# Diagonal 64x64 and 32x32 TensorE tiles in the attention stage of a fused linear-attention and mixture-of-experts kernel, blocks stored without their zeros, and 27 block sets instead of 20

## The chip, the cores and the metric

The kernel runs on one core of a Trainium2 chip. The metric is the device time of one execution in microseconds (us). TensorE (PE) multiplies matrices and writes only to PSUM; VectorE (DVE), ScalarE (ACT) and GpSimd (POOL) do the element-wise work; SyncE (SP) issues most of the DMAs. Each engine works through its own instructions in the order in which they stand; the engines wait for one another through semaphores.

## The reference

```python
def _attn_ref(r, k, v, w, a, b):            # B, H, S, D = 4, 8, 768, 40
    state = zeros((B, H, D, D))
    for t in range(S):
        y[:, :, t] = einsum('bhd,bhde->bhe', rt, state)
        Sa = einsum('bhde,bhe->bhd', state, at)
        state = state * wt[:, :, None, :] - einsum('bhd,bhe->bhde', Sa, bt)
        state = state + einsum('bhd,bhe->bhde', vt, kt)
    return y

def _moe_ref(x, w_gate, w1, w2):            # x: 3072 x 320, 8 experts, F = 1024
    P = exp(x @ w_gate - max)               # then 8 rounds of row and column normalisation
    for e in range(E):
        out += P[:, e:e+1] * (maximum(x @ w1[e], 0) @ w2[e])
```

The output of the attention, 3072 tokens of 8 x 40 values, is the input of the mixture of experts.

## The kernel before

**Two stages.** `attention` computes the recurrence, and `body` goes on with the eight experts. The experts start from `xd`, a DRAM copy of the attention's output, and use the SBUF that the attention's pools release, in the order of the pools: `stg` and `x0` lie where the attention's inputs, the inversion buffers and the first block sets were, `hp` (results of the first expert layer) over the last sets, `x1` over what comes behind.

**The recurrence in chunks.** The 768 steps are cut into 12 chunks of 64 (index `c`), for 4 batches (`b`) of 4 head pairs (`p`). The two heads of a pair lie side by side: on partitions 0 to 39 and 64 to 103 for the 40 dimensions, on 0 to 63 and 64 to 127 for the 64 steps of a chunk. Inside a chunk the recurrence is a triangular system. Three kinds of work result:

- `prep(c, b)` depends on inputs alone: two scans on DVE (`q`, `gf`), products on POOL or DVE (`kb`, `ab`), products and transposes on PE (`ll`, `kt`), and copies by ACT into a *block set* that `recur` reads later. A set has `sx` (832 columns), `bb` (the negated `b` vectors, 416 columns) and `cc`. There are `NSX` = 20 sets, used in turn. Eight of them serve at first as staging buffers for inputs (`IN_SETS`) and for `kb` and `lt` (`KB_SETS`) of the first eight preps. `first_use` (L100) clears `bb` on POOL and copies an identity into `sx` on ACT.
- The inversion: for two chunks at a time, 128 triangular 32x32 blocks are inverted on DVE (`inv_diag`, `inv_off`, L181 to L210), one block on each partition. `ld`, `ud` and `nd` are DRAM tiles that carry the blocks to that layout and back. `tload` (L212) fetches the inverted blocks, and `tmat` (L233) merges two 32x32 inverses into one 64x64 inverse with two products, `gp` and `op`, and ACT copies between and behind them. `tt` holds the result for each pair as a 128x128 matrix with one 64x64 inverse for each head on its diagonal and zeros elsewhere.
- `recur(c, b)` (L250) is the sequential part: `av`, the mask into `f` (DVE), `xc`, copies into `x1` and `c1` (ACT), `pu` = `tt` times `x1` (PE, L287), the mask into `pm` (DVE, L289), `c2` = `bb` times `pm` (PE, L294), the sum `ws` (DVE, L296), and from it the output `y` and the state `z` for the next chunk (POOL), transposed by PE (`zt`) into `vz`. One `recur` is called a step here: 48 steps.

**Products in float32.** Each product of two float32 operands stands in the trace as two LDWEIGHTS and two MATMUL records: 192 products `pu` give 384 records. A transpose gives one.

**What sets the order.** All pieces get a due time in the list `ev` and are written in that order; a scheduler that goes by its own timing of the program then sets the order on each engine, until block `N_MAN` = 8 of the experts, from where the written order holds. So a changed tile or count shifts the order of other pieces too.

**Experts.** `layer1` forms its products in seven pieces (L564), `layer2` adds into PSUM (L629). `prep_w` splits weights, `prep_x` splits inputs (`xs`, `xt`, `xch`, `xcl`) on DVE, ACT and POOL. The first `prep_x` run beside the last steps of the recurrence.

Of the kernel before, what the change touches and what calls it, by code (L numbers as in the profile page):

```python
# [29 lines left out]
def attention(ctx, tc, d, xd, ps, pq, pt, gs, lg):  # L30
    nc = tc.nc
# [17 lines left out]
    NTB = 2  # L49
    sx_b, bb_b, cc_b = ([None] * NSX for _ in range(3))  # L50
    raws = {}
    for n in range(NCH * NB - NSX, NCH * NB):
        i, pool = n % NSX, sets[n - NCH * NB + NSX]
        if i in IN_SETS or i in KB_SETS:
            raw = pool.tile([128, 1252], F32, name=f"st{i}")
            raws[i] = raw
            sx_b[i] = raw[:, 0:832].rearrange("r (p h x) -> r p h x", h=2, x=104)
            bb_b[i] = raw[:, 832:1248].rearrange("r (p x) -> r p x", x=104)
            cc_b[i] = raw[0:R2, 1248:1252]
            continue  # L60
        sx_b[i] = pool.tile([128, NP, 2, 104], F32, name=f"sx{i}")
        bb_b[i] = pool.tile([128, NP, 104], F32, name=f"bb{i}")
        cc_b[i] = pool.tile([R2, NP], F32, name=f"cc{i}")
    tt_b = [const.tile([128, 4 * NP, 128], F32, name=f"tt{i}") for i in range(NTB)]
    td_b = [const.tile([128, 4 * NP + 1, 32], F32, name="td")]
    lg_b = [const.tile([128, 4 * NP, 64], F32, name="lg")]
# [4 lines left out]
    x1_b = [const.tile([128, NP, 128], F32, name=f"x1{i}") for i in range(2)]  # L71
# [13 lines left out]
    def clear():  # L85
        nc.gpsimd.memset(unf, 0.0)
        nc.gpsimd.memset(unf[:, 0:1024:33], 1.0)
        for t in vz_b + c1_b + lg_b:
            nc.vector.memset(t, 0.0)
        for t in rb_b + f_b:  # L90
            nc.vector.memset(t[96:128], 0.0)
        nc.vector.memset(td_b[0][:, 4 * NP], 0.0)
        for t in x1_b:
            nc.vector.memset(t[:, :, 104:128], 0.0)
        nc.vector.memset(kb1[96:128], 0.0)
        for t in tt_b:
            nc.gpsimd.memset(t, 0.0)
    fresh = set(range(NSX))

    def first_use(i):  # L100
        if i in fresh:
            fresh.discard(i)
            nc.gpsimd.memset(bb_b[i], 0.0)
# [12 lines left out]
    def prep(c, b, ld):  # L116
# [16 lines left out]
        nc.vector.tensor_tensor_scan(  # L133
            out=gf.rearrange("r p t -> r (p t)")[:, 259::-1], data0=inp[:, 260:0:-1],
# [3 lines left out]
        g = gf[0:R2, :, 64:0:-1]  # L138
        if cb < NKB:
            raw = raws[KB_SETS[cb % len(KB_SETS)]]  # L140
            kb = raw[0:R2, 0:512].rearrange("r (p k t) -> r p k t", p=NP, k=2)
# [32 lines left out]
        nc.scalar.copy(out=sx[0:64, :, :, 64:104], in_=kt[0:64, :, :, 0:40])  # L174
        nc.scalar.activation(out=bb[0:64, :, 0:40], in_=kt[64:128, :, 0, 0:40], func=AF.Copy, scale=-1.0)
        nc.scalar.activation(out=bb[64:128, :, 64:104], in_=kt[64:128, :, 1, 0:40], func=AF.Copy, scale=-1.0)
# [35 lines left out]
    def tload(c):  # L212
        tt = rot("tt", tt_b)
        tts[c] = tt
        ld, ud, nd = invs[GRP[c][0]]
        t1, t2, lb = td_b[0][0:64, 0:4 * NP], td_b[0][64:128, 0:4 * NP], lg_b[0][0:64]
        cc = GRP[c][1]
        q = [slice(h * 32, h * 32 + 32) for h in range(2)]
        u = [[slice(cc * 64 + blk * 32 + h * 16, cc * 64 + blk * 32 + h * 16 + 16) for h in range(2)]
             for blk in range(2)]  # L220
        for h in range(2):
            nc.sync.dma_start(out=lb[q[h], :, q[h]],
                              in_=ld[cc, 0:32].rearrange("j b p h s -> j (b p) h s")[:, :, h, 32:64])
        for h in range(2):
            nc.sync.dma_start(out=t1[q[h]], in_=nd[u[0][h]].rearrange("g j s -> j g s"))
        for h in range(2):
            nc.sync.dma_start(out=t2[q[h]], in_=ud[u[1][h]].rearrange("g j s -> j g s"))
        for h in range(2):
            for blk in range(2):
                r = slice(h * 64 + blk * 32, h * 64 + blk * 32 + 32)  # L230
                nc.sync.dma_start(out=tt[r, :, r], in_=ud[u[blk][h]].rearrange("g j s -> j g s"))

    def tmat(c, half):  # L233
        gl = slice(half * 8, half * 8 + 8)
        tt = tts[c][:, gl]
        gw = slice(half * 8, half * 8 + 9)
        t1, t2 = td_b[0][0:64, gw], td_b[0][64:128, gw]
        lb, gs = lg_b[0][0:64, gl], lg_b[0][64:128, gl]
        gp = pt.tile([64, 2 * NP + 1, 32], F32, name="gp", tag="pt")
        for p in range(2 * NP):  # L240
            nc.tensor.matmul(gp[:, p:p + 2], lhsT=lb[:, p], rhs=t1[:, p:p + 2], start=True, stop=True)
        nc.scalar.copy(out=gs[0:32, :, 0:32], in_=gp[0:32, 0:2 * NP])
        nc.scalar.copy(out=gs[32:64, :, 32:64], in_=gp[32:64, 0:2 * NP])
        op = pt.tile([64, 2 * NP + 1, 32], F32, name="op", tag="pt")
        for p in range(2 * NP):
            nc.tensor.matmul(op[:, p:p + 2], lhsT=gs[:, p], rhs=t2[:, p:p + 2], start=True, stop=True)
        nc.scalar.copy(out=tt[0:32, :, 32:64], in_=op[0:32, 0:2 * NP])
        nc.scalar.copy(out=tt[64:96, :, 96:128], in_=op[32:64, 0:2 * NP])

    def recur(c, b):  # L250
# [16 lines left out]
        for p in range(NP):  # L267
            nc.tensor.matmul(av[:, p], lhsT=vz[:, p], rhs=rb[:, p], start=True, stop=True)
# [10 lines left out]
        x1 = rot("x1", x1_b)  # L279
        c1 = rot("c1", c1_b)  # L280
# [4 lines left out]
        pu = ps.tile([128, NP, 128], F32, name="pu", tag="ps")  # L285
        for p in range(NP):
            nc.tensor.matmul(pu[:, p], lhsT=tts[c][:, b * NP + p], rhs=x1[:, p], start=True, stop=True)  # L287
        pm = wk.tile([128, NP, 104], F32, name="pm")
        nc.vector.tensor_tensor(out=pm, in0=pu[:, :, 0:104], in1=mask_p.unsqueeze(1).broadcast_to([128, NP, 104]),  # L289
                                op=ALU.mult)  # L290
        yield
        c2 = ps.tile([R2, NP, 104], F32, name="c2", tag="ps")
        for p in range(NP):
            nc.tensor.matmul(c2[:, p], lhsT=pp["bb"][:, p], rhs=pm[:, p], start=True, stop=True)  # L294
        ws = wk.tile([R2, NP, 104], F32, name="ws")
        nc.vector.tensor_tensor(out=ws, in0=c2, in1=c1, op=ALU.add)  # L296
# [45 lines left out]
    preps, invs, tts, gd, ys = {}, {}, {}, {}, {}  # L342
# [477 lines left out]
```

## Time and profile before

| | |
|---|---|
| median of 3 runs | 1844.17 us (1842.89 to 1850.96) |
| the profiled execution | 1846.42 us, of which the span of the profile is 1844.6 us |
| granted TensorE clock, mean | 0.969 |
| busy share of the span | PE 93%, DVE 76%, POOL 48%, ACT 46% |
| first `pu` of the recurrence | 110.8 us |
| last `c2` of the recurrence | 519.2 us |

The recurrence runs from 111 to 520 us, prepared in the first 110 us; the rest belongs to the experts. In the profile, L with a number is a line of the kernel, PEld are the weight loads of TensorE, `out<-in` are the names of the written and read tiles, and a number behind "idle before" is how long the engine stood still ahead of the group, with what released it. A matmul's row shows a length that includes its way through the array; how close products follow each other is read from their starts.

### The profile page before, as it was taken

How to read it: one execution, taken by the hardware profiler on the slowest of the kernel's cores; microseconds unless marked ns; L12 is line 12 of the kernel's file. 1: busy time of each engine (PE TensorE's matmuls, PEld its weight loads, DVE VectorE, ACT ScalarE, POOL GpSimd, SP SyncE). 2: the span in 40 equal slices, each digit the busy share in tenths (PEclk: the TensorE clock that was granted, in tenths of full speed). 3: DMA queues.
4: the chain of work that ended last, by engine and by line, in shares of the span. 5: the costliest groups of instructions: out<-in, count | busy, mean ns of one | idle time of the engine just before them, and what ended most of it. 6: DMA issues, size and time to landing. Idle time of an engine off the chain costs nothing.

```text
span 1844.6 us, 31499 instructions
## 1 busy us (share of the span) xinstructions
PE 1717.9 (93%) x11843; PEld 1684.3 (91%) x11843; DVE 1395.4 (76%) x2315; ACT 855.9 (46%) x1848; POOL 882.4 (48%) x848
## 2 busy tenths in 40 slices
PE   4478898888989999999999999999999999999999
PEld 4368788888878999999999999999999999999999
DVE  7877979777598868677776868977686877767675
ACT  6357576675643534344343433445343443425342
POOL 6545655441573618355371826007191744628170
PEclk8579899999999999999999999999999999999999
DMA  8477787885730102011110202201020111102001
GB/s 211 117 169 160 175 201 178 178 179 129 188 95 31 56 2 74 21 55 38 38 56 19 75 20 68 66 12 57 20 75 20 56 38 38 57 19 75 5 34 43
DMA packets 194957, 145.10 MB, mean 79 GB/s; under 512 B 143861, under 2 KB 171637, under 8 KB 194805
## 3 DMA queue, kind: packets, MB, share of 16 engines
q1 hardware_dynamic: 191125, 137.35, 28.6%
q10 hardware_dynamic: 3680, 5.74, 1.1%
q8 instruction: 94, 1.54, 0.4%
q14 instruction: 58, 0.48, 0.1%
HBM read 117.00 MB, written 26.04 MB: 78 GB/s over the span
## 4 chain that ended last, share of the span: by engine, by line
PE 72%; DVE 13%; DMA 4%; issue 3%; POOL 3%; ACT 1%; SPq 1%; DVEq 0%; ACTq 0%; POOLq 0%
PE op L629 36%; PE p L564 33%; DVE pr L193 2%; DVE gt L196 2%; DMA inp<-in_inp_dram 1%; DVE un L196 1%; DVE q L123 1%; POOL kb L147 1%; DVE gf L133 1%; PE xc L276 1%; PE ll L159 1%; DMA ld<-lt 1%; DMA xs<-xd 1%; POOL ab L154 1%; DVE sm L582 1%
## 5 line engine op out<-in xcount | busy, mean ns | idle before, releaser
L564 PE MATMUL p<-xch,wh 128*128 128x384 f32 (+1 forms) x1792 | 604.8, 339 | 9.5 <-DVE sm L582 5.6
L585 ACT ACTIVATE hh<-sm 128x384 fp32r<-128x384 f32 x512 | 269.4, 527 | 723.2 <-DVE sm L582 723.2
L629 PE MATMUL op<-wh,hh 128*128 128x320 f32 x1536 | 476.4, 311 | 1.0 <-ACT hh L585 0.9
L629 PE MATMUL op<-wl,hh 128*128 128x320 f32 x1536 | 474.2, 309 | 0.0
L629 PE MATMUL op<-wh,hl 128*128 128x320 f32 x1536 | 466.7, 309 | 0.8 <-DVE hl L588 0.8
L510 POOL TENSOR_TENSOR wl<-ws,wh 128x640 fp32r<-128x640 f32 x60 | 103.1, 1718 | 605.6 <-ACT wh L508 605.4
L588 DVE SCALAR_TENSOR_TENSOR hl<-sm,hh 128x384 fp32r<-128x384 f32 x512 | 373.4, 763 | 2.4 <-ACT hh L585 2.0
L564 PEld LDWEIGHTS p<-xch,wh 128*128 128x128 f32 (+1 forms) x1792 | 336.8, 188 | 13.7 <-DVE sm L582 6.8
L564 PE MATMUL p<-xcl,wh 128*128 128x384 f32 x896 | 302.2, 337 | 0.0
L564 PE MATMUL p<-xch,wl 128*128 128x384 f32 x896 | 301.5, 337 | 0.0
L629 PEld LDWEIGHTS op<-wh,hh 128*128 128x128 f32 x1536 | 289.9, 189 | 1.6 <-ACT hh L585 1.5
L629 PEld LDWEIGHTS op<-wl,hh 128*128 128x128 f32 x1536 | 290.7, 189 | 0.0
L629 PEld LDWEIGHTS op<-wh,hl 128*128 128x128 f32 x1536 | 286.4, 188 | 1.2 <-DVE hl L588 1.0
L582 DVE TENSOR_TENSOR sm<-p,u 128x384 f32<-128x384 f32 x384 | 233.0, 617 | 8.8
L582 DVE TENSOR_TENSOR sm<-p,p 128x384 f32<-128x384 f32 x128 | 71.3, 557 | 129.0 <-PE p L564 74.4
L564 PEld LDWEIGHTS p<-xcl,wh 128*128 128x128 f32 x896 | 168.4, 188 | 0.0
L564 PEld LDWEIGHTS p<-xch,wl 128*128 128x128 f32 x896 | 168.4, 188 | 0.0
L582 DVE TENSOR_TENSOR p<-p,p 128x384 f32<-128x384 f32 x128 | 71.1, 556 | 101.6 <-PE p L564 101.2
L582 DVE TENSOR_TENSOR u<-p,p 128x384 f32<-128x384 f32 x128 | 70.8, 553 | 57.2 <-PE p L564 56.0
L159 PE MATMUL ll<-ab,kb 128*128 128x128 f32 x336 | 60.8, 335 | 48.3 <-POOL ab L154 23.2
L518 POOL TENSOR_TENSOR wl<-ss,wh 128x512 fp32r<-128x512 f32 x60 | 89.7, 1495 | 30.1 <-ACT wh L515 25.9
L159 PEld LDWEIGHTS ll<-ab,kb 128*128 128x128 f32 x336 | 52.3, 237 | 54.1 <-POOL kb L147 27.2
(161 smaller groups left out, 2747.3 us busy)
## 6 DMA issues: line engine op xcount, KB each, us to landing
ws<-in_wts_dram SPq DMA_DIRECT2D x60, 832.0 KB
inp<-in_inp_dram SPq DMA_DIRECT2D x42, 450.2 KB
rb<-in_r_dram SPq DMA_DIRECT2D x48, 224.0 KB
gd<-gf SPq DMA_DIRECT2D x48, 113.8 KB
gr<-gd SPq DMA_DIRECT2D x48, 113.8 KB
vz<-in_v_dram SPq DMA_DIRECT2D x48, 112.0 KB
ld<-lt ACTq DMA_DIRECT2D x40, 128.0 KB
f<-in_vt_dram SPq DMA_DIRECT2D x48, 80.0 KB
```

What stands on the lines that cost most here:

```text
L123: nc.vector.tensor_tensor_scan(out=qf.rearrange("r p t -> r (p t)"), data0=inp[:, 0:260], data1=one65, initial=0.0, op0=ALU.mult, op1=ALU.add)
L133: nc.vector.tensor_tensor_scan(out=gf.rearrange("r p t -> r (p t)")[:, 259::-1], data0=inp[:, 260:0:-1], data1=g1.rearrange("r p t -> r (p ...
L159: nc.tensor.matmul(ll[:, p], lhsT=kb[:, p], rhs=ab[0:kb.shape[0], p], start=True, stop=True)
L193: nc.vector.tensor_tensor(out=prv, in0=a.unsqueeze(3).broadcast_to([nu, n_c, n_k, n_r]), in1=m.unsqueeze(1).broadcast_to([nu, n_c, n_k, n_ ...
L196: nc.vector.tensor_reduce(out=dst, in_=prv.rearrange("u c k r -> u c r k"), op=ALU.add, axis=AX.X)
L510: g.tensor_tensor(out=wl[:, 0:640], in0=raw[:, 256:896], in1=wh[:, 0:640], op=ALU.subtract)
L518: g.tensor_tensor(out=lv[:, 3:7], in0=so[:, :, 0], in1=hv[:, 3:7, 0], op=ALU.subtract)
L564: nc.tensor.matmul(o, lhsT=w_, rhs=x_, start=(j == 0), stop=(j == 3))
L582: eng.tensor_tensor(out=out, in0=x, in1=y, op=ALU.add)
L585: nc.scalar.activation(out=hh[:, f, h], in_=sm[f][:, h], func=AF.Relu)
L588: v.scalar_tensor_tensor(out=hl[:, f, h], in0=sm[f][:, h], scalar=0.0, in1=hh[:, f, h], op0=ALU.max, op1=ALU.subtract)
L629: nc.tensor.matmul(ops[i], lhsT=a[:, h, cs], rhs=w_[:, cw], start=(f == 0 and h == 0 and j == 0), stop=(last and h == 1 and j == 2))
```

## The change

**Products.** `pu` and `c2` were four products each over the full array, with block-diagonal weights. Each is now eight products, one for each head of each pair, with both operands on partitions 0 to 63 or 64 to 127 and the result on the same ones: the two tiles on the diagonal of TensorE. `gp` and `op` were eight 64x64 products each per half chunk (with two neighbours of `td` as moving operand); each is now sixteen 32x32 products.

**Storage.** With no block-diagonal weights, `tt` shrinks from 128 to 64 columns for a pair, `lg` from 64 to 32, `x1` from 128 to 104, and `bb` from 416 to 184 (160 of data and 24 that are cleared since the last head reads 64 columns). `gp` goes back with one ACT copy instead of two.

**Clearing.** `lg`, the spare column of `td` and the tail of `x1` are no longer cleared by DVE; `first_use` clears 24 columns instead of 416.

**Sets.** `NSX` is 27. The staging sets are now 19 to 26, so the preps of the first 19 sets write to memory that was no staging buffer.

```diff
-            raw = pool.tile([128, 1252], F32, name=f"st{i}")
+            raw = pool.tile([128, 1032], F32, name=f"st{i}")
...
+        else:
+            raw = pool.tile([128, 1020], F32, name=f"st{i}")
+        sx_b[i] = raw[:, 0:832].rearrange("r (p h x) -> r p h x", h=2, x=104)
+        bb_b[i] = raw[:, 832:1016]
+        cc_b[i] = raw[0:R2, 1016:1020]
+    tt_b = [const.tile([128, 4 * NP, 64], F32, name=f"tt{i}") for i in range(NTB)]
+    td_b = [const.tile([128, 4 * NP, 32], F32, name="td")]
+    lg_b = [const.tile([128, 4 * NP, 32], F32, name="lg")]
...
-        for t in vz_b + c1_b + lg_b:
+        for t in vz_b + c1_b:
             nc.vector.memset(t, 0.0)
...
-        nc.vector.memset(td_b[0][:, 4 * NP], 0.0)
-        for t in x1_b:
-            nc.vector.memset(t[:, :, 104:128], 0.0)
...
-            nc.gpsimd.memset(bb_b[i], 0.0)
+            nc.gpsimd.memset(bb_b[i][:, 160:184], 0.0)
...
         for p in range(2 * NP):
-            nc.tensor.matmul(gp[:, p:p + 2], lhsT=lb[:, p], rhs=t1[:, p:p + 2], start=True, stop=True)
-        nc.scalar.copy(out=gs[0:32, :, 0:32], in_=gp[0:32, 0:2 * NP])
-        nc.scalar.copy(out=gs[32:64, :, 32:64], in_=gp[32:64, 0:2 * NP])
+            for r in (0, 32):
+                nc.tensor.matmul(gp[r:r + 32, p], lhsT=lg[r:r + 32, p], rhs=td[r:r + 32, p], start=True, stop=True)
+        nc.scalar.copy(out=lg[64:128], in_=gp)
...
+            for h in range(2):
+                r = slice(64 + h * 32, 96 + h * 32)
+                nc.tensor.matmul(op[h * 64:h * 64 + 32, p], lhsT=lg[r, p], rhs=td[r, p], start=True, stop=True)
...
-            nc.tensor.matmul(pu[:, p], lhsT=tts[c][:, b * NP + p], rhs=x1[:, p], start=True, stop=True)
+            for h in hs:
+                nc.tensor.matmul(pu[h, p], lhsT=tts[c][h, b * NP + p], rhs=x1[h, p], start=True, stop=True)
...
-            nc.tensor.matmul(c2[:, p], lhsT=pp["bb"][:, p], rhs=pm[:, p], start=True, stop=True)
+            for h in hs:
+                nc.tensor.matmul(c2[h, p], lhsT=pp["bb"][h, p * 40:p * 40 + 64], rhs=pm[h, p], start=True, stop=True)
...
-NSX = 20
+NSX = 27
...
-IN_SETS = (19, 18, 17, 16)
-KB_SETS = (15, 14, 13, 12)
-IN_SEQ = (19,18,17,16,0,0,19,18)
+IN_SETS = (26, 25, 24, 23)
+KB_SETS = (22, 21, 20, 19)
+IN_SEQ = (26, 25, 24, 23, 0, 0, 26, 25)
```

**The order, on PE.** Near the end of the recurrence, where `gp` and `op` of the last chunk stand among the steps, PE had before (x4 is a group of four products; `lp` is the gate's product, `kt` and `ll` belong to a prep and are past):

```order
L316 MATMUL zt<-cst,z 40x104 x4
L326 MATMUL lp<-gs,y 128x8 x3
L294 MATMUL c_5164<-pm,bb_187 104x104 x4
L241 MATMUL gp<-td,lg 64x64 x8
L287 MATMUL pu<-x_213,tt_202 128x128 x4
L276 MATMUL xc_5183<-f_208,sx_192 104x104 x4
L276 MATMUL xc_5184<-f_208,sx_192 104x104 x4
L246 MATMUL op<-td,lg 64x64 x4
L268 MATMUL av<-rb_211,vz_217 104x128 x4
L246 MATMUL op<-td,lg 64x64 x4
```

and now, in the same part of the last chunks:

```order
L315 MATMUL zt<-cst,z 40x104 x4
L293 MATMUL c_5975<-pm,st_201 64x104 x8
L285 MATMUL pu<-x_218,tt_206 64x104 x7
L242 MATMUL op<-td,lg 32x32 x16
L285 MATMUL pu<-x_218,tt_206 64x104
L272 MATMUL xc_5999<-f_213,st_203 104x104 x4
L272 MATMUL xc_6000<-f_213,st_203 104x104 x4
L264 MATMUL av<-rb_216,vz_222 104x128 x4
```

The small products alone left the full array before; now `c2` and `pu`, which mostly follow each other, do so too. Over the whole attention stage the form of the tile changes 148 times before (74 stretches of 64x64) and 247 times now.

**The order, on POOL.** Among the preps of the first chunks, POOL had before:

```order
L154 TENSOR_TENSOR ab_205<-st_176,gf 40x4x64
L103 MEMSET st_170 128x416
L152 COPY cc_200<-q 104x4
L103 MEMSET st_169 128x416
L153 TENSOR_TENSOR ab_206<-st_175,gf 40x4x64
L154 TENSOR_TENSOR ab_206<-st_175,gf 40x4x64
L103 MEMSET st_176 128x416
L103 MEMSET st_172 128x416
L103 MEMSET st_175 128x416
L147 TENSOR_TENSOR kb<-st_175,q 104x512
```

and now:

```order
L149 TENSOR_TENSOR ab_209<-st_183,gf 40x4x64
L147 COPY st_191<-q 104x4
L98 MEMSET st_203 128x24
L148 TENSOR_TENSOR ab_210<-st_182,gf 40x4x64
L149 TENSOR_TENSOR ab_210<-st_182,gf 40x4x64
L98 MEMSET st_183 128x24
L98 MEMSET st_182 128x24
L98 MEMSET st_179 128x24
L142 TENSOR_TENSOR kb<-st_182,q 104x512
```

The place is the same; five clears of 416 columns ahead of `kb` have become four of 24.

**The order, on DVE.** Where the recurrence ends and the experts' inputs are prepared (`xt`, `xcl`, `xch` belong to `prep_x`), DVE had before:

```order
L269 TENSOR_TENSOR f_210<-av,cst 104x8x64
L296 TENSOR_TENSOR ws<-c_5288,c_222 104x416
L550 TENSOR_TENSOR xcl_5426<-xt,xch_5425 128x4x128
L552 TENSOR_TENSOR xch_5425<-xt,xch_5425 32x4x128
L289 TENSOR_TENSOR pm<-pu,cst 128x416
L330 COPY lg<-lp 128x8
L296 TENSOR_TENSOR ws<-c_5325,c_221 104x416
L582 TENSOR_TENSOR sm_5526<-p_5546,p_5528 128x384
```

and now:

```order
L549 TENSOR_TENSOR xcl_6191<-xt,xch_6190 128x4x128
L551 TENSOR_TENSOR xch_6190<-xt,xch_6190 32x4x128
L265 TENSOR_TENSOR f_214<-av,cst 104x8x64
L295 TENSOR_TENSOR ws<-c_6026,c_226 104x416
L287 TENSOR_TENSOR pm<-pu,cst 128x416
L329 COPY lg<-lp 128x8
L295 TENSOR_TENSOR ws<-c_6071,c_225 104x416
L287 TENSOR_TENSOR pm<-pu,cst 128x416
```

The last two operations of the first `prep_x` stand two places earlier, ahead of the last `f`. Elsewhere on DVE the inversions of chunks 2 and 3 end behind the third `ws` instead of the fifth, those of chunks 4 to 7 and of 10 and 11 one `ws` earlier than before, those of chunks 8 and 9 at the same one.

More of the change, by code (lines that the diff above doesn't have):

```diff
@@ L54, in attention @@
         if i in IN_SETS or i in KB_SETS:
-            raw = pool.tile([128, 1252], F32, name=f"st{i}")
+            raw = pool.tile([128, 1032], F32, name=f"st{i}")
             raws[i] = raw
[L57 to L66, printed above, removed]
+        else:
[6 more added lines that the diff above has]
+    lg_b = [const.tile([128, 4 * NP, 32], F32, name="lg")]
     ab_b = [pin.tile([128, NP, 128], F32, name=f"ab{i}") for i in range(2)]
@@ L70, in attention @@
     rb_b = [io.tile([128, NP, 128], F32, name=f"rb{i}") for i in range(NRB)]
-    x1_b = [const.tile([128, NP, 128], F32, name=f"x1{i}") for i in range(2)]
+    x1_b = [const.tile([128, NP, 104], F32, name=f"x1{i}") for i in range(2)]
     g1_b = [pin.tile([RP, NP, 65], F32, name=f"g1{i}") for i in range(1)]
@@ L174, in prep @@
         nc.scalar.copy(out=sx[0:64, :, :, 64:104], in_=kt[0:64, :, :, 0:40])
-        nc.scalar.activation(out=bb[0:64, :, 0:40], in_=kt[64:128, :, 0, 0:40], func=AF.Copy, scale=-1.0)
-        nc.scalar.activation(out=bb[64:128, :, 64:104], in_=kt[64:128, :, 1, 0:40], func=AF.Copy, scale=-1.0)
+        for h in range(2):
+            nc.scalar.activation(out=bb[h * 64:h * 64 + 64, 0:160].rearrange("s (p x) -> s p x", x=40),
+                                 in_=kt[64:128, :, h, 0:40], func=AF.Copy, scale=-1.0)
         if cb >= NKB:
@@ L215, in tload @@
         ld, ud, nd = invs[GRP[c][0]]
-        t1, t2, lb = td_b[0][0:64, 0:4 * NP], td_b[0][64:128, 0:4 * NP], lg_b[0][0:64]
+        t1, t2, lb = td_b[0][0:64], td_b[0][64:128], lg_b[0][0:64]
         cc = GRP[c][1]
@@ L221, in tload @@
         for h in range(2):
-            nc.sync.dma_start(out=lb[q[h], :, q[h]],
+            nc.sync.dma_start(out=lb[q[h]],
                               in_=ld[cc, 0:32].rearrange("j b p h s -> j (b p) h s")[:, :, h, 32:64])
@@ L229, in tload @@
             for blk in range(2):
-                r = slice(h * 64 + blk * 32, h * 64 + blk * 32 + 32)
-                nc.sync.dma_start(out=tt[r, :, r], in_=ud[u[blk][h]].rearrange("g j s -> j g s"))
+                nc.sync.dma_start(out=tt[h * 64 + blk * 32:h * 64 + blk * 32 + 32, :, blk * 32:blk * 32 + 32],
+                                  in_=ud[u[blk][h]].rearrange("g j s -> j g s"))
     def tmat(c, half):
@@ L235, in tmat @@
         tt = tts[c][:, gl]
[L236 to L239, printed above, removed]
+        td, lg = td_b[0][:, gl], lg_b[0][:, gl]
+        gp = pt.tile([64, 2 * NP, 32], F32, name="gp", tag="pt")
         for p in range(2 * NP):
-            nc.tensor.matmul(gp[:, p:p + 2], lhsT=lb[:, p], rhs=t1[:, p:p + 2], start=True, stop=True)
-        nc.scalar.copy(out=gs[0:32, :, 0:32], in_=gp[0:32, 0:2 * NP])
-        nc.scalar.copy(out=gs[32:64, :, 32:64], in_=gp[32:64, 0:2 * NP])
-        op = pt.tile([64, 2 * NP + 1, 32], F32, name="op", tag="pt")
+            for r in (0, 32):
+                nc.tensor.matmul(gp[r:r + 32, p], lhsT=lg[r:r + 32, p], rhs=td[r:r + 32, p], start=True, stop=True)
+        nc.scalar.copy(out=lg[64:128], in_=gp)
+        op = pt.tile([96, 2 * NP, 32], F32, name="op", tag="pt")
         for p in range(2 * NP):
-            nc.tensor.matmul(op[:, p:p + 2], lhsT=gs[:, p], rhs=t2[:, p:p + 2], start=True, stop=True)
-        nc.scalar.copy(out=tt[0:32, :, 32:64], in_=op[0:32, 0:2 * NP])
-        nc.scalar.copy(out=tt[64:96, :, 96:128], in_=op[32:64, 0:2 * NP])
+            for h in range(2):
+                r = slice(64 + h * 32, 96 + h * 32)
+                nc.tensor.matmul(op[h * 64:h * 64 + 32, p], lhsT=lg[r, p], rhs=td[r, p], start=True, stop=True)
+        for h in range(2):
+            nc.scalar.copy(out=tt[h * 64:h * 64 + 32, :, 32:64], in_=op[h * 64:h * 64 + 32])
     def recur(c, b):
@@ L284, in recur @@
         yield
-        pu = ps.tile([128, NP, 128], F32, name="pu", tag="ps")
+        pu = ps.tile([128, NP, 104], F32, name="pu", tag="ps")
+        hs = [slice(h * 64, h * 64 + 64) for h in range(2)]
         for p in range(NP):
-            nc.tensor.matmul(pu[:, p], lhsT=tts[c][:, b * NP + p], rhs=x1[:, p], start=True, stop=True)
+            for h in hs:
+                nc.tensor.matmul(pu[h, p], lhsT=tts[c][h, b * NP + p], rhs=x1[h, p], start=True, stop=True)
         pm = wk.tile([128, NP, 104], F32, name="pm")
-        nc.vector.tensor_tensor(out=pm, in0=pu[:, :, 0:104], in1=mask_p.unsqueeze(1).broadcast_to([128, NP, 104]),
+        nc.vector.tensor_tensor(out=pm, in0=pu, in1=mask_p.unsqueeze(1).broadcast_to([128, NP, 104]),
                                 op=ALU.mult)
         yield
-        c2 = ps.tile([R2, NP, 104], F32, name="c2", tag="ps")
+        c2 = ps.tile([128, NP, 104], F32, name="c2", tag="ps")
         for p in range(NP):
-            nc.tensor.matmul(c2[:, p], lhsT=pp["bb"][:, p], rhs=pm[:, p], start=True, stop=True)
+            for h in hs:
+                nc.tensor.matmul(c2[h, p], lhsT=pp["bb"][h, p * 40:p * 40 + 64], rhs=pm[h, p], start=True, stop=True)
         ws = wk.tile([R2, NP, 104], F32, name="ws")
-        nc.vector.tensor_tensor(out=ws, in0=c2, in1=c1, op=ALU.add)
+        nc.vector.tensor_tensor(out=ws, in0=c2[0:R2], in1=c1, op=ALU.add)
         if b % 2 == 0:
```

## The prediction

> **What bounds the kernel now.** I read the table by stages first, since the average hides that the program has two.
>
> ```profile
> span 1844.6 us, 31499 instructions
> ...
> core 0: us, PE busy (x) PEld busy (x) DVE busy (x) ACT busy (x) POOL busy (x), PEclk, DMA share, GB/s
> 184.00:230.00 46.00, 38.40 (x341) 35.76 (x340) 42.28 (x61) 26.84 (x67) 27.76 (x28) 0.89 0.77 176
> 322.00:368.00 46.00, 40.47 (x392) 38.17 (x390) 35.67 (x58) 30.31 (x77) 19.95 (x25) 0.93 0.85 180
> 368.00:415.00 47.00, 41.45 (x413) 38.53 (x412) 33.25 (x57) 33.22 (x84) 23.66 (x27) 1.00 0.81 175
> 600.00:1844.00 1244.00, 1238.63 (x7778) 1236.36 (x7776) 919.36 (x1577) 502.57 (x990) 571.42 (x491) 1.00 0.13 42
> ```
>
> From 600 us on PE is busy 1238.6 of 1244 us, at the full granted clock (1.00). The change touches nothing there, so whatever it does happens in the first 520 us. In the recurrence two engines take turns. From 184 to 230 us, where an inversion runs, DVE is busy 42 of 46 us (92%); from 322 to 415 us DVE falls to 71 to 78% and PE stands at 88%. The chain of waits, second, agrees:
>
> ```profile
> by line: issue 10.2%; DVE pr L193 7.3%; DVE gt L196 6.8%; DMA inp<-in_inp_dram 6.3%; DVE un L196 5.7%; POOL kb L147 3.9%; DVE q L123 3.9%; PE xc L276 3.4%; DVE gf L133 3.1%; PE ll L159 2.5%; DVE pm L289 2.4%; DVE ws L296 2.2%; PE av L268 2.
> ```
>
> Between 110 and 521 us its largest engine entries are the inversion (L193 and the two of L196, 19.8% together); of PE's products `xc`, `ll` and `av` appear, each under 4%, and `pu`, `c2`, `gp`, `op` not at all. So I let half of a PE saving or loss in the recurrence reach the end.
>
> **Products: the pace.** Third comes one stretch in order of time in which PE never pauses, with ACT's copy of `gp` ahead and one `gp` group from elsewhere behind:
>
> ```profile
> L243 ACT COPY lg<-gp 32x256 f32<-32x256 f32 x24 | 8.7, 362 | 0.3
> ...
> 388.15 1.04 PE L268 MATMUL av<-rb,vz 128*104 128x128 f32 x8
> 389.03 0.52 PE L316 MATMUL zt<-cst,z 104*40 104x104 f32 x4
> 389.39 0.90 PE L294 MATMUL c<-pm,bb 128*104 128x104 f32 x8
> 390.12 1.08 PE L159 MATMUL ll<-ab,kb 128*128 128x128 f32 x8
> 391.03 0.52 PE L167 MATMUL kt<-cst,kb 104*128 104x104 f32 x4
> 391.39 1.08 PE L287 MATMUL pu<-x,tt 128*128 128x128 f32 x8
> 392.31 1.63 PE L276 MATMUL xc<-f,sx 128*104 128x104 f32 x16
> 393.77 1.04 PE L268 MATMUL av<-rb,vz 128*104 128x128 f32 x8
> 394.74 0.68 PE L241 MATMUL gp<-td,lg 64*64 64x64 f32 x8
> 395.34 1.16 PE L159 MATMUL ll<-ab,kb 128*128 128x128 f32 x8
> 396.34 0.52 PE L167 MATMUL kt<-cst,kb 104*128 104x104 f32 x4
> ...
> 174.85 1.11 PE L241 MATMUL gp<-td,lg 64*64 64x64 f32 x16
> 175.89 0.98 PE L276 MATMUL xc<-f,sx 128*104 128x104 f32 x8
> ```
>
> From start to start, 8 records of `pu` (128 columns) take 392.31 - 391.39 = 0.92 us, 0.115 each; 8 of `c2` (104 columns) 390.12 - 389.39 = 0.73, 0.091 each. For `gp` (64 columns) 8 take 0.60 and 16 take 1.04 us, so 8 more cost 0.44, 0.055 each. The pace follows the columns.
>
> **Do two tiles run at once?** The change doubles the records: 16 for each `pu` and each `c2`, 32 for each `gp` and `op` of a half chunk. One place bears on it: at 109 us `op` (partitions 64 to 127) and `gp` (0 to 63) met.
>
> ```profile
> 108.38 0.97 PE L246 MATMUL op<-td,lg 64*64 64x64 f32 x13
> 109.13 0.27 PE L241 MATMUL gp<-td,lg 64*64 64x64 f32 x1
> 109.18 0.22 PE L246 MATMUL op<-td,lg 64*64 64x64 f32 x1
> 109.24 0.22 PE L241 MATMUL gp<-td,lg 64*64 64x64 f32 x1
> 109.24 0.22 PE L246 MATMUL op<-td,lg 64*64 64x64 f32 x1
> 109.30 0.22 PE L241 MATMUL gp<-td,lg 64*64 64x64 f32 x1
> 109.30 0.22 PE L246 MATMUL op<-td,lg 64*64 64x64 f32 x1
> 109.35 0.92 PE L241 MATMUL gp<-td,lg 64*64 64x64 f32 x13
> ```
>
> Two records start at 109.24 and two at 109.30: each tile keeps its pace of 0.055 to 0.06 us while the other runs. So I take two diagonal tiles as two streams.
>
> - `pu`: 8 records a stream at the pace of 104 columns, 8 x 0.091 = 0.73 instead of 0.92 us; 48 times -0.19 is **-9 us of PE**.
> - `c2`: 0.73 as before, **0**.
> - `gp`, `op`: 16 records a stream. If the pace goes on falling with the columns, 32 columns take 0.0275 us, 0.44 for a group instead of 0.88; if the pair at 109.24 is already the fastest issue (two in 0.058), 32 records take 0.93. I take the middle, 0.69, since the column law has three rows and the issue limit one; 48 groups times -0.19 is **-9**, between -21 and +2.
>
> The Trainium skill (TensorEngine Tiling (Array Packing), Gotcha 1: PSUM Pressure) says that different row tiles cannot write the same PSUM bank at a time. The two that met above wrote two banks; the diagonal pairs write one, on different partitions, which no row here shows. It is the rival "single file" below.
>
> **What the change of form costs.** The same stretch gives it. `av` ahead of `gp` lasts 394.74 - 393.77 = 0.97 instead of 389.03 - 388.15 = 0.88 us; the `gp` group 0.60 instead of 0.44; `ll` behind it 396.34 - 395.34 = 1.00 instead of 391.03 - 390.12 = 0.91. One stay in the 64x64 form costs 0.09 + 0.16 + 0.09 = 0.34 us, 0.17 a change. The form changes 148 times before and 247 times now: 99 x 0.17 = **+17 us of PE**. A direct step from 32 to 64 (47 of them) may cost less; with those at nothing it is (247 - 47 - 148) x 0.17 = +9.
>
> The Trainium skill (TensorEngine Tiling (Array Packing), Key Properties) says that changing the tiling mode drains TensorE. The rows agree and give the price, 0.17 us.
>
> PE together: -9 + 0 - 9 + 17 = -1 us, between -9 - 21 + 9 = -21 and -9 + 2 + 17 = +10. Half of it reaches the end: **-0.5**, between -10.5 and +5.
>
> **The start.** Until the first `q` everything waits for DVE's clears, then POOL stands ahead of a prep.
>
> ```profile
> 5.46 0.91 DVE L89 MEMSET lg<- 128x1024 f32 x1 [0.16 <-issue]
> 6.52 1.02 DVE L91 MEMSET rb<- 32x512 f32 x2
> 10.24 0.09 DVE L92 MEMSET td<- 128x32 f32 x1
> 10.68 0.48 DVE L95 MEMSET kb<- 32x512 f32 x1
> 11.20 0.70 DVE L123 TENSOR_TENSOR_SCAN q<-st,cst 112x260 f32<-112x260 f32 x1
> L123 DVEq EVENT_SEMAPHORE  x1: 21/21/21, 6.5 to 6.5; - x1
> 13.74 0.42 ACT L174 COPY sx<-kt 64x320 f32<-64x320 f32 x1 [5.05 <-PE kt L167]
> ...
> 9.73 0.21 POOL L466 MEMSET ones<- 128x128 f32 x1
> 40.10 0.45 POOL L103 MEMSET st<- 128x416 f32 x1
> 41.00 0.83 POOL L103 MEMSET st<- 128x416 f32 x2 [0.46 <-DMA ld<-st]
> 41.91 1.18 POOL L147 TENSOR_TENSOR kb<-st,q 104x512 f32<-104x512 f32 x1
> ```
>
> Without `lg`, `td` and `x1`, DVE saves (6.52 - 5.46) + (10.68 - 10.24) = 1.5 us ahead of `q`, whose semaphore event is over at 6.5 us, so nothing else holds it. On POOL a clear of 416 columns takes 0.45 us; one of 24 lies below the 0.21 of 128 columns, so the three ahead of `kb` at 41.9 us save about 0.9, less what the wait for `ld` (0.46) keeps: between 0 and 1.3, I take **1**. In sum **-2.5**, between -1 and -2.8. Seven more identity copies on ACT cost nothing while ACT waits for the first transposes, 5 us long.
>
> **ACT and the hand-over.** `gp`'s copy is one instead of two: 24 x 0.36 = 8.7 us of ACT. With 33 of 47 us busy at most, ACT hides most of that, between 0 and -2: **-1**. Two operations of `prep_x` stand ahead of the last `f` now instead of behind two later pieces; the same work in another order, 0, between -2 and +2 (its two operations take under 2 us). The 27 sets: no wait of a prep for a released set is among the listed waits of the recurrence, so **0** from the memory itself. The span that the order shifts is at most a step, 409 us / 48 = 8.5 us.
>
> **Sum.** 1844.6 - 0.5 - 2.5 - 1 = 1840.6 us of span. The profiled execution is 1846.4 by the metric, 2.2 above the median of the runs; -4 from the median 1844.2 gives **1840 us**. A change under 0.5%, 9.2 us, cannot be told from none here.
>
> **The rivals.**
>
> - *Cheap small tiles.* `gp` and `op` go on at the column pace and direct steps between 32 and 64 cost nothing: PE -21, and the stretches of 322 to 415 us pass half on: 1844 - 10.5 - 3.5 = **1830**. For it: the pace falls evenly over three widths. Against it: the chain names none of these products.
> - *A step gained by the order.* Four of five inversions end one or two `ws` earlier in DVE's order. If the recurrence waits for them at one place, a step goes: 1840 - 8.5 = **1832**. For it: 20% of the chain are inversions. Against it: DVE has the same work, and what is put behind comes later.
> - *Single file.* The pairs share a PSUM bank and run one after the other. `pu` takes 16 x 0.091 = 1.46 (+0.54), `c2` +0.73, 48 times 1.27 = +61; with +17 of changes and nothing gained at `gp` PE has +78 us more; half is +39: 1844 + 39 - 3.5 = **1880**, slower. It decides as soon as a second tile's record starts 0.09 instead of under 0.01 us behind the first. For it: no row shows one bank. Against it: the streams at 109 us.
> - *The changes on the path.* Each step now holds a change into and out of the 64x64 form between `x1` and `ws`, which the step's own chain waits for: all +17 reaches the end, the shorter `pu` and `gp` stay hidden: 1844 + 17 - 3.5 = **1857**. For it: PE at 88% and its long gaps rather than its pace would have to hide them. Against it: half of the recurrence hangs on DVE.
>
> **How the numbers follow.** Forecast 46%, its own range 1832 to 1850; cheap small tiles 19%; order 10%; single file 11%; changes on the path 14%. Faster than 1835: most of the second and third and a tenth of the first, 0.31. Slower than 1853.4: the single file, two thirds of the last case, a little of the first, 0.21. Within: 0.48. The range takes in everything but the single file and the ends of the others: **1826 to 1857**.
>
> **What would show it.** Right: `pu` and `c2` of 16 records in about 0.75 us each from start to start, with two records starting together; a stay costing about 0.3 us; the first `q` near 9.7 us; a first expert product as late as before within 5 us. Wrong: 1.4 us for a group (single file); groups of `gp` of 0.45 us (cheap tiles); inversions that start several us earlier while PE's groups are as forecast (order); PE's pauses of the recurrence unchanged but its busy time up by 15 us (changes on the path). After 600 us the profile should be the same as before; if it is not, the forecast has missed a whole part.

## The result: 0.7% slower, and the profile after

The changed kernel takes 1861.46 us (median of 6 runs, 1857.49 to 1865.25) against 1848.70 us of the kernel before in the same comparison (6 runs, 1842.89 to 1850.96): ratio 1.0074, interval 1.0053 to 1.0095, so 12.8 us slower. The forecast was 1840 us, range 1826 to 1857; it started from the median of three runs of the kernel before, 1844.17 us, which lies 4.5 us below that of the six.

The table by stages of the changed kernel, same columns as the one of before:

```profile
span 1858.7 us, 34584 instructions
...
core 0: us, PE busy (x) PEld busy (x) DVE busy (x) ACT busy (x) POOL busy (x), PEclk, DMA share, GB/s
184.00:230.00 46.00, 39.06 (x557) 34.97 (x556) 43.12 (x67) 30.50 (x77) 26.68 (x32) 0.93 0.80 182
322.00:368.00 46.00, 36.44 (x496) 33.35 (x495) 31.47 (x57) 30.34 (x77) 23.04 (x29) 0.93 0.86 187
368.00:415.00 47.00, 39.53 (x537) 36.06 (x537) 33.73 (x45) 29.41 (x75) 21.53 (x24) 0.86 0.70 162
600.00:1844.00 1244.00, 1241.01 (x7790) 1238.95 (x7790) 923.77 (x1588) 504.28 (x994) 572.09 (x492) 1.00 0.13 42
```

From 600 us on nothing has changed: PE is as full as before (1241.0 of 1244 us), at full clock. The span has grown by 14.1 us, and the sum `ws` that ends each step says where; the view of one tile gives count, shortest/median/longest ns, and first and last start, first of before, then of after:

```profile
L296 DVE TENSOR_TENSOR ws<-c,c x48: 549/582/620, 120.0 to 519.5; 104x416 f32<-104x416 f32 x48
```

```profile
L295 DVE TENSOR_TENSOR ws<-c,c x48: 555/584/601, 130.9 to 532.8; 104x416 f32<-104x416 f32 x48
```

The recurrence begins 10.9 us late and ends 13.3 us late. The products are not the reason. Here is PE in the changed kernel without a pause, with most of a `gp` group near the top:

```profile
388.56 1.12 PE L264 MATMUL av<-rb,vz 128*104 128x128 f32 x8
389.61 0.43 PE L236 MATMUL gp<-td,lg 32*32 32x32 f32 x14
389.97 0.54 PE L315 MATMUL zt<-cst,z 104*40 104x104 f32 x4
390.44 0.93 PE L293 MATMUL c<-pm,st 64*64 64x104 f32 x16
391.20 0.88 PE L285 MATMUL pu<-x,tt 64*64 64x104 f32 x16
392.01 0.69 PE L242 MATMUL op<-td,lg 32*32 32x32 f32 x32
```

From start to start 16 records of `c2` take 0.76 us (8 took 0.73 before), 16 of `pu` 0.81 (8 took 0.92), and 32 of `op` are over within 0.69 us, where 16 took 1.04 and more. So two tiles run at once, and a record of 32 columns costs about 0.02 us. The medians over all groups that run on without a pause at full clock, worked out from the starts and with the changes of form in them, went from 0.73 to 0.76 us for `c2`, 0.97 to 0.81 for `pu`, 1.07 to 0.62 for `op`: 48 times (+0.03 - 0.16 - 0.45) is **28 us less work for PE** in these groups (`gp` and `op` are 48 together, and `gp` is put down like `op`). Of the groups beside them `zt` alone grew clearly, from 0.36 to 0.45 us, which takes some 4 us back over its 44 groups.

What grew is DVE's idle time. The windows of the recurrence for DVE alone, before (110 to 520 us) and after (110 to 533 us); behind the length stand its busy time and its instructions:

```profile
110.00:520.00 410.00, 323.37 (x479) 0.95 0.74 172
```

```profile
110.00:533.00 423.00, 320.26 (x473) 0.89 0.72 167
```

The work is the same, 323 and 320 us; the idle time went from 86.6 to 102.7 us. The waits of DVE in the same stretches, before and then after (us in total, times, longest):

```profile
DVE f L269 <- PE av L268: 26.3, 11, 5.6
DVE pr L184 <- DMA lu<-ld: 13.2, 4, 5.2
DVE ws L296 <- PE c L294: 11.8, 13, 1.7
DVE q L123 <- DMA inp<-in_inp_dram: 9.4, 5, 3.9
```

```profile
DVE f L265 <- PE av L264: 31.2, 16, 6.4
DVE ws L295 <- PE c L293: 18.5, 16, 2.4
DVE q L118 <- DMA inp<-in_inp_dram: 14.9, 5, 5.6
DVE lg L329 <- PE lp L325: 11.1, 10, 4.2
DVE st L164 <- PE ll L154: 8.7, 7, 1.8
```

The inversions no longer wait for their DMA (13.2 us gone), and most of the others wait more. Shorter products that are waited for longer point to where the instructions stand. At the start this can be seen on DVE, before and after:

```profile
113.80 1.54 DVE L133 TENSOR_TENSOR_SCAN gf<-inp,g 112x260 f32<-112x260 f32 x1
115.26 0.56 DVE L289 TENSOR_TENSOR pm<-pu,cst 128x416 f32<-128x416 f32 x1
```

```profile
113.45 1.53 DVE L128 TENSOR_TENSOR_SCAN gf<-inp,g 112x260 f32<-112x260 f32 x1
...
120.00 1.08 DVE L192 TENSOR_REDUCE gt<-pr 128x64 f32<-128x512 f32 x1
120.99 0.59 DVE L287 TENSOR_TENSOR pm<-pu,cst 128x416 f32<-128x416 f32 x1
```

The first `pm` stood right behind `gf`; now eight pieces of the second inversion and the `q`, `g` and `gf` of a prep stand between them. A second difference is the granted clock. The windows of 110 to 535 us, before and after:

```profile
110.00:535.00 425.00, 367.68 (x3430) 343.72 (x3428) 337.26 (x497) 277.30 (x680) 219.37 (x242) 0.96 0.73 170
```

```profile
110.00:535.00 425.00, 360.28 (x4847) 325.80 (x4847) 321.83 (x476) 258.89 (x638) 200.97 (x234) 0.89 0.72 166
```

In these traces the granted clock is 1.00 or 0.50 and nothing between, so a mean of 0.96 is 2 x 0.04 x 425 = 34 us at half clock, 0.89 is 94 us (a mean of two digits leaves 4 us open either way). Two theories: **order** (the scheduler laid the pieces out anew, and the new order is the slower one) and **clock** (lighter products let TensorE fall to half clock more often, which gives the saving back).

### The profile page after: what moved, and what is told of

It reads as the page before. It is cut to its first block, busy times and chain, and to the rows that moved or that the text cites. A ratio compares the mean times of both kernels' runs of the same rounds, so it can differ in the third digit from the quotient of the medians.

```text
span 1858.7 us, 34584 instructions
## 1 busy us (share of the span) xinstructions
PE 1721.5 (93%) x13379; PEld 1675.7 (90%) x13379; DVE 1395.5 (75%) x2311; ACT 849.3 (46%) x1831; POOL 865.4 (47%) x855
## 4 chain that ended last, share of the span: by engine, by line
PE 73%; DVE 10%; DMA 6%; issue 4%; POOL 3%; SPq 2%; ACT 2%; POOLq 0%; DVEq 0%; ACTq 0%
PE op L628 35%; PE p L563 33%; DVE pr L189 1%; DVE gt L192 1%; DMA xs<-xd 1%; DVE un L192 1%; DVE gf L128 1%; DMA ld<-lt 1%; PE xc L272 1%; POOL ab L148 1%; DMA inp<-in_inp_dram 1%; PE ll L154 1%; DVE q L118 1%; PE c L293 1%; PE pu L285 1%
```

## The experiments

All ratios are to the kernel before, with the 95% interval. To set an order, a table of instruction numbers was added behind the program, with a dependency without a semaphore from each instruction to the next on its engine; the instructions themselves stay those of the changed kernel:

```diff
         body(tc, d, out)
+        _set_order(tc, nc)    # all five engines, one list each
```

### The change in the order of the kernel before

> The changed kernel's instructions, put on every engine into the order that the kernel before had. Theory 'order' (the 13 us were lost because the scheduler laid the pieces out anew, the first step's mask pm behind pieces of the second inversion above all): last ws back at 519 us or earlier, first ws near 120 us, time 1838 to 1849 us (ratio 0.994 to 1.000). Theory 'clock' (the lighter products leave TensorE idle in more of the clock's windows, and the half clock gives the saving back, whatever the order): half-clock time within the recurrence stays near 90 us (before 41), time 1855 to 1866 us.

Measured: 1850.58 us, ratio 1.0009 (0.9995 to 1.0022). So the order makes 10.9 us of the loss: that much lies between the same instructions in the two orders. Its steps run as those of before, on a lighter PE and a slower clock; first the view of `ws`, then the windows of all engines:

```profile
L295 DVE TENSOR_TENSOR ws<-c,c x48: 552/582/593, 120.7 to 522.2; 104x416 f32<-104x416 f32 x48
```

```profile
110.00:535.00 425.00, 369.83 (x4913) 334.10 (x4911) 334.66 (x495) 267.59 (x654) 216.93 (x240) 0.90 0.72 170
```

The first `ws` comes at 120.7 us (before 120.0), and the 41st at 469.2 (before 470.3): 28 us less of PE's work and 85 instead of 34 us at half clock leave the steps where they were. The last comes 2.7 us later. PE's busy time did not fall here, 369.8 after 367.7 us: the slower clock took up what the lighter products saved. So this run alone does not show that time on PE is worth nothing. The time is 1.6 us above what 'order' expected and 4.4 below 'clock'; the half-clock time is what 'clock' said. So the order has most of it, and whether the clock has the rest is the next question.

### Filling TensorE's waits, in both orders

In 38 and 35 places where TensorE had stood still for 0.8 us or more, products of the identity were put ahead, written into the tile that the next real product overwrites:

```diff
+    def warm(name, tile, m, n, sub=""):
+        ...
+        for _ in range(WARM.get(f"{name}{seen[name]}{sub}", 0)):
+            nc.tensor.matmul(tile, lhsT=ident[:, 0:m], rhs=ident[:, 0:n], start=True, stop=True)
...
+        warm("av", av[:, 0], 104, 128)
         for p in range(NP):
             nc.tensor.matmul(av[:, p], lhsT=vz[:, p], rhs=rb[:, p], start=True, stop=True)
```

> The changed kernel in its own order, with 226 products that nobody reads (about 51 us at full clock) in 38 places where TensorE stood still for 0.8 us or more between 112 and 535 us. Theory 'clock': half-clock time in the recurrence falls from 92 us to 60 or less, last ws at 518 to 526 us, time 1846 to 1855 us. Theory 'order': the waits have other causes than the clock, so the recurrence ends at 532 us or later, time 1858 to 1868 us.

> The change in the order of the kernel before (1850.6 us), with 160 products that nobody reads (some 36 us at full clock) in 35 places where TensorE stood still for 0.8 us or more between 112 and 525 us. If the half clock costs time there: half-clock time between 110 and 535 us falls from 89 to 50 us or less, and time to 1842 to 1847 us. If it is only a sign of waiting: 1849 to 1854 us.

Measured: 1866.45 us (1.0104, 1.0089 to 1.0120) in the change's order, and 1850.66 us (1.0014, 1.0001 to 1.0027) in the old one. The windows of 110 to 535 us of the first, then of the second:

```profile
110.00:535.00 425.00, 390.14 (x5296) 356.92 (x5296) 319.34 (x477) 259.02 (x638) 198.06 (x234) 0.95 0.72 166
```

```profile
110.00:535.00 425.00, 382.49 (x5224) 347.35 (x5224) 339.23 (x496) 268.34 (x655) 224.32 (x244) 0.96 0.72 170
```

The clock came back to that of before (0.95 and 0.96; 43 and 34 us at half clock). The time did not: 5 us more in the new order, nothing in the old one (1850.66 against 1850.58). The half clock was a sign of waiting, not what cost the time. In the second run PE is busy for 382.5 us, of which some 36 are fillers: about 21 us less of the kernel's own work than before, at the same clock, and by the medians the end did not come earlier. One limit: the fillers are not pure, since some wait themselves for the PSUM tile that they write (those ahead of `av` 9.0 us in the first run). The second run's profiled execution has a span of 1842.0 us, 6.7 less than that without fillers, but the medians of 12 and 11 runs agree: a single profiled execution lies some us off the median either way.

### Where in the order the loss is made

Two kernels change the order at the end of the second inversion: old order first, then the change's, and the reverse.

```diff
 # the second kernel is the reverse, with 156 us
-the change's order on every engine
+what the kernel before had begun by 166 us, in its order; then the rest in the change's order
```

> The changed kernel with the order of the kernel before up to the end of the second inversion (166 us), and its own order from there on. If the loss is made at the start (first ws at 130.9 instead of 120.0 us) and carried to the end: first ws near 120 us, time 1846 to 1853 us. If it is made by the later order or by the clock: 1857 to 1865 us.

> The reverse: the changed kernel's own order up to the end of the second inversion (156 us), then the order of the kernel before. If the loss is made at the start: first ws near 131 us, time 1857 to 1864 us. If by the later order: 1845 to 1852 us. Theory 'clock': 1855 to 1866 us here and in the run with the old start alike.

Measured: 1856.99 us (1.0056, 1.0039 to 1.0074) and 1858.25 us (1.0056, 1.0043 to 1.0068). Read alone, the first run says 'the later order' and the second 'the start'; both lie in the range of 'clock' too (1855 to 1866), so that what speaks against the clock are the runs above. Either part of the new order costs 6 to 8 us against 1850.6, and both together 10.9. The first of the two shows that the visible late start isn't needed for a loss: 

```profile
L295 DVE TENSOR_TENSOR ws<-c,c x48: 558/578/593, 119.6 to 528.2; 104x416 f32<-104x416 f32 x48
```

Its steps begin at 119.6 us and still end 8.7 us later than before. So I moved the three DVE instructions that make the start late, and nothing else: the first `pm` behind `gf`, the third `f` and the first `ws` behind the next pieces, as before. VectorE's list:

```diff
 gf
+pm (first)
 pr, un (diag), pr (diag), q, un (diag), g, pr (diag), gf
+f (third)
 un (diag)
+ws (first)
 pr, gt (off)
-pm (first)
 pr (off)
-f (third)
 ...
-ws (first)
```

> The change in its own order, with three VectorE instructions of the first steps moved ahead to where the kernel before has them relative to the second inversion: the first pm, the third f and the first ws. If the stall that is seen at 112 to 131 us is what makes the change slower: first ws near 121 us instead of 130.9 and time 1850 to 1854 us. If the steps behind it wait for other pieces of the order anyway: first ws early, fourth ws and the end as in the change, time 1857 to 1863 us.

Measured: 1862.35 us (1.0093, 1.0068 to 1.0118). `ws` of this run, the first, the second and the third:

```profile
120.36 0.59 DVE L295 TENSOR_TENSOR ws<-c,c 104x416 f32<-104x416 f32 x1
...
140.74 0.58 DVE L295 TENSOR_TENSOR ws<-c,c 104x416 f32<-104x416 f32 x1
...
150.12 0.56 DVE L295 TENSOR_TENSOR ws<-c,c 104x416 f32<-104x416 f32 x1
```

The first step ends 10.5 us earlier, the second where it did (140.2 in the change), and the last at 535.3 (532.8). The most striking stall of the trace was worth nothing by itself. The second `pm` kept its place in VectorE's list, behind the same pieces of the inversion, so this run tests the one stall and not the whole start.

### Which part of the change moves the order

The two parts alone, each in the order that the scheduler gives it. First `pu` and `c2` on diagonal tiles with the small storage and 26 sets, as many as fit, and the products of `gp` and `op` as before; second the kernel before, with its 20 sets, and only `gp` and `op` changed:

```diff
 # the change, with the merges of before
-            for r in (0, 32):
-                nc.tensor.matmul(gp[r:r + 32, p], lhsT=lg[r:r + 32, p], rhs=td[r:r + 32, p], start=True, stop=True)
+            nc.tensor.matmul(gp[:, p:p + 2], lhsT=lb[:, p], rhs=t1[:, p:p + 2], start=True, stop=True)
 # the kernel before, with the merges of the change
-            nc.tensor.matmul(gp[:, p:p + 2], lhsT=lb[:, p], rhs=t1[:, p:p + 2], start=True, stop=True)
+            for r in (0, 32):
+                nc.tensor.matmul(gp[r:r + 32, p], lhsT=lg[r:r + 32, p], rhs=td[r:r + 32, p], start=True, stop=True)
```

> One part alone, in the order that the scheduler gives it: pu and c2 on the diagonal tiles with the small storage, gp and op as 64x64 products as before (26 sets, which is what fits). VectorE's order has the first pm at place 165 (the change 152, before 145). If pu and c2 are what moved the order: first ws later than 125 us, time 1857 to 1867 us. If gp and op did: 1845 to 1852 us.

> The other part alone, in the scheduler's order: the kernel before (20 sets, full-array pu and c2, blocks with zeros) with gp and op as 32x32 products. The first pm stands at place 146 on VectorE. If pu and c2 moved the order: first ws near 121 us, time 1844 to 1851 us. If gp and op did: 1856 to 1864 us.

Measured: 1862.99 us (1.0091, 1.0065 to 1.0118) and **1842.06 us (0.9973, 0.9960 to 0.9986)**, the latter faster than both kernels. So the slow order comes with `pu` and `c2`, their storage and the sets; which of these brings it is not shown, since no run changes one of them alone. The first `ws` of the first kernel came at 134.1 us, as expected. Of the second expectation both numbers failed: the time lies below 1844 to 1851, and the first `ws` came at 126.3 us, not 121. Its last came at 514.0, 5.5 us before that of the kernel before; again the start does not decide alone.

Two runs altered one number of the due times, in the change and in the merges alone:

```diff
-P0 = -8
+P0 = -7
```

> The change with one number of the order's due times altered: P0, the lead of the preps, is -7 instead of -8; all products and tiles as in the change. First pm at place 149. If the place of the pieces in the order is what sets the time: it differs from the change's 1861 us by over 5 us, and first ws comes before 127 us. If the products or the clock set it: 1858 to 1865 us.

> The new merges alone with the lead of the preps P0 at -7 instead of -8, in the scheduler's order. With the full change this number was worth 7 us. If it is worth something of itself: 1833 to 1839 us. If each order is its own case: anything within 10 us of the 1842 us without it, on either side.

Measured: 1854.25 us (1.0036, 1.0022 to 1.0051), 7.2 us better than the change, and 1853.46 us (1.0035, 1.0021 to 1.0048), 11.4 us worse than the merges alone. In the first of the two `ws` begins at 127.2 us, just behind the 127 that was expected; the second misses the 10 us of its own expectation by 1.4. The number has no worth of its own; each order is a case of its own, with a spread of some 10 us either way. A later place of the first `pm` mostly went with a longer time (145 before, 149 in the change with -7, 152 in the change, 165 in the first part alone), but it does not tell which order is good: 146 stands for 1842 and for 1853 us, and `pm` moved with two others gained nothing.

### The whole change in the good order

```diff
-_set_order: none (the scheduler's)
+_set_order: the lists of the merges alone, which took 1842 us
```

> The whole change (pu and c2 on diagonal tiles, small blocks, 27 sets) put on every engine into the order of the run with the new merges alone, which took 1842 us. If the diagonal tiles of pu and c2 neither cost nor bring anything once the order is given: 1839 to 1846 us, ratio to the kernel before 0.995 to 0.999. If they cost by themselves (more changes of tile form, more half clock): 1848 us or more.

Measured: 1844.17 us (0.9983, 0.9969 to 0.9997). The same instructions that took 1861.5 us in the scheduler's order take 17.3 us less here. Against the merges alone in that order (1842.06) the diagonal tiles of `pu` and `c2`, with their storage and sets, bring nothing; the intervals meet. The first `ws` of both runs, the merges alone ahead, come at about the same time; the last of the profiled executions lie 7 us apart, of which the medians show 2:

```profile
L295 DVE TENSOR_TENSOR ws<-c,c x48: 548/582/609, 126.3 to 514.0; 104x416 f32<-104x416 f32 x48
L295 DVE TENSOR_TENSOR ws<-c,c x48: 549/586/600, 125.8 to 521.0; 104x416 f32<-104x416 f32 x48
```

### What sets the pace, if not TensorE

The change in the old order, with VectorE's contractions (`pr`, `gt` and `un` of `inv_off`) over half of their terms; the other half of each sum is left out:

```diff
     def contract(us, dst, a, m):
         nu = us.stop - us.start
+        a, m = a[:, :, 0:a.shape[2] // 2], m[:, 0:m.shape[1] // 2]
```

> The changed kernel in the order of the kernel before, with the contractions of the inversion (the products pr and the sums gt and un of inv_off) over half of their terms, which leaves out half of that sum and some 60 us of VectorE's work beside the recurrence. If VectorE's work sets the pace of the recurrence there: last ws at 505 us or earlier instead of 522, time 1828 to 1838 us. If the chain of the steps and the standing order set it whatever the engines' load: last ws at 517 us or later, time 1845 to 1852 us.

Measured: 1809.91 us (0.9800, 0.9783 to 0.9817), 40.7 us less than with all terms, and well below the 1828 to 1838 that were expected. The contractions from 60 to 535 us (busy us, mean ns; the last number is idle time ahead), first with all terms:

```profile
L192 DVE TENSOR_REDUCE un<-pr 128x64 f32<-128x512 f32 (+2 forms) x24 | 47.9, 1994 | 0.1
L192 DVE TENSOR_REDUCE gt<-pr 128x64 f32<-128x512 f32 (+2 forms) x24 | 45.8, 1907 | 0.2
L189 DVE TENSOR_TENSOR pr<-gt,un 128x512 f32<-128x512 f32 (+2 forms) x24 | 30.3, 1261 | 0.1
L189 DVE TENSOR_TENSOR pr<-un,lu 128x512 f32<-128x512 f32 (+2 forms) x24 | 30.1, 1256 | 0.1
```

And with half of the terms, where the products and the operands of the sums have half the elements; the view of `ws` follows:

```profile
L193 DVE TENSOR_REDUCE un<-pr 128x64 f32<-128x256 f32 (+2 forms) x24 | 25.4, 1057 | 0.1
L193 DVE TENSOR_REDUCE gt<-pr 128x64 f32<-128x256 f32 (+2 forms) x24 | 24.5, 1019 | 0.2
L190 DVE TENSOR_TENSOR pr<-gt,un 128x256 f32<-128x256 f32 (+2 forms) x24 | 19.3, 805 | 0.1
L190 DVE TENSOR_TENSOR pr<-un,lu 128x256 f32<-128x256 f32 (+2 forms) x24 | 18.0, 749 | 0.1
```

```profile
L296 DVE TENSOR_TENSOR ws<-c,c x48: 552/591/599, 110.8 to 484.0; 104x416 f32<-104x416 f32 x48
```

DVE loses 154.1 - 87.2 = 66.9 us of work, and 41 us of it, 0.6, reach the end: 9.9 us at the first `ws` (120.7 to 110.8), the rest by the last (522.2 to 484.0). In the same order 28 us less of PE's work, at a slower clock, reached it with nothing. Along a standing order it is DVE's pieces that set the pace of the recurrence. Whether they do so by the engine's time or because the inverted blocks come earlier, this run does not tell apart.

## Why the prediction was wrong, step by step

- **What bounds the kernel**: right on the stage (nothing changes after 600 us), wrong on the share. "I let half of a PE saving or loss in the recurrence reach the end": with the order held it was none, twice (+2.2 us for -28 us of PE in the old order, with an interval of -0.9 to +4.1; +2.1 for `pu` and `c2`, with their storage and sets, in the merges' order). The same chain of waits that I quoted named DVE's inversions at 20% and none of the changed products; that was the better guide than DVE at 71 to 78% and PE at 88%.
- **Products**: two streams at once was right, and so was 0.75 us for a group (0.76 and 0.81). The term that was mis-sized is the +17 us for 99 more changes of form, beside -18 for the pace of all groups: the groups with their changes measured -28, and `zt` +4. A group of 32 records takes 0.62 us, between the 0.44 and 0.93 that were given and near the 0.69 that was taken, and the direct changes cost hardly anything: `c2`, `pu` and `op` follow each other at 390.44, 391.20 and 392.01. Around a `gp` alone the price is there (`av` ahead of it 389.61 - 388.56 = 1.05 instead of 0.88 us, `zt` between it and `c2` 0.47 instead of 0.36). It cost the forecast little, since with the order held nothing of it is seen at the end.
- **Single file** fell: pairs that write one PSUM bank on different partitions run together, 32 records of `op` within 0.69 us, and 16 of `c2` within about the time of 8 before. The Trainium skill (TensorEngine Tiling (Array Packing), Gotcha 1: PSUM Pressure) says that different row tiles cannot use one PSUM bank at a time. In this trace that does not hold for the diagonal tiles.
- **Cheap small tiles** had it right that direct changes cost next to nothing, but its sign, groups of 0.45 us, did not come (0.62), and neither did its time of 1830.
- **Changes on the path** comes near by its number, 1857, and by that alone. Its sign, PE busy for 15 us more, did not come (360.3 after 367.7 us from 110 to 535 us), and the same tiles took 1850.6 and 1844.2 us in two other orders.
- **The start**: right at its place, and worth nothing at the end. The timeline of DVE in the change:

```profile
9.15 0.48 DVE L90 MEMSET kb<- 32x512 f32 x1
9.66 0.70 DVE L118 TENSOR_TENSOR_SCAN q<-st,cst 112x260 f32<-112x260 f32 x1
```

The first `q` starts at 9.66 us (9.7 forecast, 11.2 before). In the old order the first `ws` still stands at 120.7 us, before 120.0.
- **The order is the step that failed.** It stood in the sum at 0, with "at most a step, 8.5 us", and only its gain was made a rival (1832, 10%). It cost 10.9 us, and the merges alone gained 5.1 in their order, though there the order and the lighter merges are not told apart. The loss as a mechanism with its own chance was missing on the slow side, where "single file" and "changes on the path" stood instead; a forecast of 1840 with 8.5 us lost would have said 1848.5, so the size was short too.
- **ACT, hand-over, 27 sets**: no sign of their own. With 27 sets and the old order the time is about that of 20 sets; the sets were not tried alone.
- **The base**: the 1840 us start from 1844.2, and the six runs of the comparison put the kernel before at 1848.7. Of the 21.5 us between forecast and result 4.5 are this, 4.2 the forecast gain, and 12.8 the loss.

Open: why one order is 10 us better than another. It is not the one stall (the three moved instructions gained nothing), not the first step, and not only one half. How the scheduler's own timing comes to put `pm` later, and whether the products, the storage or the sets move it, stays open too.

## What to carry to other kernels

Before a saving on one engine is costed, hold the order fixed and ask which engine's work the end follows: here 67 us less on VectorE gave 41 us, and 28 us less on TensorE gave nothing. Where a scheduler sets the order, a change of the instruction list can draw a new order, which was worth some 10 us in this kernel (the same instructions took 1861.5, 1850.6 and 1844.2 us in three orders), more than the edit itself; run the new code in the old order before judging the edit, and keep the better order. A stall that leaps to the eye, or a clock that falls, may be where waiting shows rather than where it comes from.

## What the hardware showed unexpectedly

Two streams of 32x32 products on diagonal tiles issue a record about every 0.02 us: 32 in 0.62 us from start to start, so 0.039 us a record for each stream, after 0.055 at 64 columns in one stream. The pace went on falling below 64 columns, though less than the columns.

With lighter products in the same order TensorE's clock was lower: 34 us at half clock in the recurrence became 85. In the recurrence of both kernels the clock stands at half for 3.41, 6.83 or 10.24 us at a time, once, twice or three times 3.41. Here is one fall in the changed kernel, the stretch ahead of it and the first at half clock (length, PE busy and its records, granted clock, DMA share, GB/s):

```profile
378.32:381.73 3.41, 1.84 (x18) 1.00 0.79 158
381.73:385.14 3.41, 3.41 (x36) 0.50 0.87 194
```

In the kernel before, the clock fell from full to half eight times between 110 and 535 us. In the 3.41 us ahead of the fall PE was busy for half of the time or less in seven cases (0 in one, 0.35 to 0.50 in six) and for 0.71 in the eighth. In the changed kernel it fell 16 times, behind shares of 0 to 0.69. A sharp limit does not come out of these figures. The Trainium skill (TensorE: Matmul & The Clock Gate, Part 1: The HAM clock gate) has a window of this length and speaks of idle ones. In these traces partly filled windows went ahead of most falls. With fillers in TensorE's waits the clock came back (0.89 to 0.95, and 0.90 to 0.96 in the old order), and the time did not.
